# Pooled scores of a unit's two heads: one step that issues both heads' products alternately, in place of a step for each head

## The chip, the cores and the metric

One core of a Trainium2 chip runs the kernel. The metric is the device time of one execution in microseconds; the time before is the median of three runs.

## The reference

Queries, keys and values have 8 batches, 8 heads, 576 positions and 64 features, all in float32. For each head the reference adds up two attentions and then runs a gated feed-forward network (FFN) on the result:

```
q_d, k_d, v_d = mean over 4 neighbouring positions      # 144 pooled positions
out_up  = repeat(softmax(q_d k_d^T / 8) v_d, 4)         # pooled attention
out_loc = softmax(masked q k^T / 8) v                   # only |i - j| < 4
x = out_up + out_loc           # reshaped to 4608 tokens x 512 features
out = (sigmoid(x w_gate) * (x w_val)) w_out             # 512 -> 1536 -> 512
```

The change touches one product only: the pooled scores q_d k_d^T, a 144 x 144 matrix for each head.

## The kernel before

**Attention.** A unit is one batch and a pair of heads, so there are 32 units, numbered 0 to 31, four to a batch. The 64 features of a unit's first head lie on partitions 0 to 63, those of its second head on partitions 64 to 127. `unit_steps` (L414) gives the steps of a unit, each of them a small function: `s0` and `s1` (the local scores, tile `s`, in two parts of 6 and 4 blocks), `sm` (the local softmax), `d0` and `d1` (the pooled scores of the first and of the second head, tile `sd`), `dn` (the pooled softmax's division), `a0` and `a1` (the transposes of the local weights, tile `at`, in two parts), `at` (the transposes of the pooled weights, tile `adt`), `od` (the pooled output), `x` (the local output in two parts, tile `x`, its sum with the pooled output, and the split of the sum into two float16 halves in `xT`).

`s_down(h)` (L505) is the step of one head. It takes a PSUM bank, issues two products of 64 rows, 72 columns and 144 moving columns (`product`, L397), and empties the bank: a maximum on VectorE (L515), its scaling on ScalarE (L516), and two exponentials with their sums on ScalarE (L518). A float32 product stands in the trace as two weight loads and two matmuls, so that a head makes four of each.

**PSUM.** The pool `ps_o` has one bank for each of its tags: `gate`, `val` and `o0` to `o3`, which the FFN uses. The pool `ps_a` has two banks under the tag `att`. The helper `bank` (L449) gives a unit of the first batch the banks `o0` to `o3`; for units 4 to 31 every tile of the attention (`s`, `sd`, `at`, `adt`, `od`, `x`, and `mxt`, the tile of a batch's maximum of the values) comes out of the two `att` banks. A tile can begin when a bank has been emptied by its last reader.

**FFN.** `moe_gate`, `moe_val` and `moe_out` work on 9 chunks of 512 tokens and 12 slices of the hidden width; each call is 12 matmuls of 512 columns. Chunk c needs `xT` of all units of the batches that its tokens come from: chunk 2 needs units 0 to 11, chunk 3 units 0 to 15, and so on to chunk 7, which needs all 32.

**Order.** The table `T` gives each step a position: for units 12 to 31 the unit's base is 82.05 plus 8.17 for each unit after the twelfth, and `m_` entries are offsets from it (L714 to L735). A slice of the FFN takes three positions, one for each of its calls, and `run_steps` puts the attention's steps between the calls. With the offsets of `T` the order in the program is, for a unit and the one before it: `s0`, `a0` of the unit before, `s1`, `d0`, then (once in a batch) `mxt`, then `a1` and `at` of the unit before, `d1`, then `od` and `x` of the unit before. This order is a wish only: the context is opened with `schedule_with_timeline_sim=True` (L866), and so an own timeline of instructions and banks settles, when the program is built, which instruction stands where on each engine. Where a step's bank isn't free in that timeline, FFN matmuls are put ahead of it. On the chip each engine then follows that fixed order and waits where data or a bank isn't ready.

In the first batch, where little other work is there, `awake` adds short matmuls on zeros after some steps (`k_` entries of `T`: three after `d0`, none after `d1`).

Of the kernel before, what the change touches and what calls it, by code (L numbers as in the profile page):

```python
# [16 lines left out]

T = dict(ma=4.5, mas=0.45, mb=9.5, mbs=0.5, c1=56, gs=2.66, g0=16.84, r1=1.99, rs=1.6, ob=3.16, v0=15.13, v1=16.62, v2=17.5, vs=2.12, o0=18, os=1.2, pro=2.36, u4=13.82, u5=21, u6=27, u7=32, l4=1.3, l5=2.77, l6=9.47, l7=8.68, lv=15.08, vm=1.58, b8=6.75, s8=6.63, b12=26.05, s12=8.17, hold=32.07, al=0.76, am=1, z=3.68, sd=0, sn=0.79, v0m=0.61, xd=[2, 3, 7], ad=[0, 3, 7], aa=[0, 1, 2, 3, 6], td=[0, 3, 9, 10], vd=[0, 1, 2, 3, 6, 9, 10], a_prep1=-2.43, a_prep2=-0.89, a_s0=0.01, a_s1=0.52, a_sm=1.82, a_d0=2.39, a_d1=2.6, a_dn=5.17, a_a0=4.37, a_vd=4.6, a_a1=5.1, a_v=2.74, a_at=5.22, a_od=5.79, a_x=8.38, m_prep0=-3.14, m_prep1=-1.14, m_prep2=-1.43, m_s0=0.69, m_s1=2.59, m_sm=3.12, m_d0=2.84, m_d1=5.8, m_a0=10, m_dn=10.78, m_vd=11.67, m_a1=12, m_v=13.07, m_at=13.44, m_od=15.64, m_x=17, k0=30, k_prep1=4, k_prep2=0, k_s0=2, k_s1=2, k_sm=4, k_d0=3, k_d1=0, k_dn=0, k_a0=3, k_vd=8, k_a1=2, k_v=5, k_at=0, k_od=0, k_x=0)  # L20
# [10 lines left out]
SD = S // 4  # L31
QM = SD // 2
# [15 lines left out]
QKSCALE = 1.0 / 8  # L48
# [10 lines left out]
def attention_moe(ctx, tc, qk, qkd, v, vd, wg, wv, wo, mask, out):  # L59
# [234 lines left out]
    vm = {}  # L294
# [119 lines left out]
    def unit_steps(u):  # L414
# [34 lines left out]
        def bank(own, name):  # L449

            if u < NPAIR:
                return ps_o.tile([P, 512], F32, tag=own, name=name)
            return ps_a.tile([P, 512], F32, tag="att", name=name)
# [48 lines left out]
            x = vdraw[u].rearrange("p a b f -> p (a b) f")  # L502
            sum4([(ps, VDB[ps, :, ps]) for ps in HALVES], x, nc.vector if u in T["vd"] else nc.gpsimd)

        def s_down(h):  # L505
            pt = bank(f"o{h}", f"sd_{u}_{h}")
            hs = slice(h * 64, h * 64 + 64)
            for qb in range(2):
                o, rows = pt[:QM, qb * SD : (qb + 1) * SD], slice(qb * QM, (qb + 1) * QM)
                product(o, [s["qd"][hs, rows]], [s["kd"][hs]])  # L510
            if h == 0:
                s["e"] = wk.tile([QM, 2, 2, SD], F32, tag="e", name=f"e_{u}", bufs=1)
                s["sme"] = wk.tile([QM, 4], F32, tag="sme", name=f"sme_{u}")
            mx = wk.tile([QM, 2], F32, tag="mxd", name=f"mxd_{u}_{h}")
            nc.vector.tensor_reduce(mx, pt[:QM, : 2 * SD].rearrange("p (q c) -> p q c", q=2), axis=AX.X, op=ALU.max)  # L515
            nc.scalar.activation(mx, mx, AF.Copy, scale=-QKSCALE / 16)  # L516
            for qb in range(2):
                nc.scalar.activation(s["e"][:, qb, h, :], pt[:QM, qb * SD : (qb + 1) * SD], AF.Exp,  # L518
                                     bias=mx[:, qb : qb + 1], scale=QKSCALE / 16,
                                     accum_out=s["sme"][:, 2 * qb + h : 2 * qb + h + 1])  # L520

        def norm_down():
            own(ad, u)
# [70 lines left out]
        def xsplit():  # L594
# [11 lines left out]

        return dict(
            prep0=lambda: None, prep1=prep1, prep2=prep2, s0=p1, s1=p2, sm=p2b,
            d0=lambda: s_down(0), d1=lambda: s_down(1), dn=norm_down,
            vd=vdsum, v=plain_v if plain else vsplit,  # L610
            a0=lambda: t_local(0, 3), a1=lambda: t_local(3, 5), at=t_down, od=av_down,
            x=lambda: (av_local(0, 8), av_local(8, 10), xsplit()),
# [258 lines left out]
```

## Time and profile before

| | us |
|---|---|
| time, median of 3 runs | 1146.84 |
| the runs | 1142.59, 1146.84, 1147.35 |
| span of the profiled execution | 1140.5 |
| PE (matmul) busy | 1093.5, 96% |
| DVE, ACT, POOL busy | 528.8, 516.9, 335.9 |
| pooled-score matmuls (`sd`) busy | 46.3, 256 instructions |
| share of `sd` in the chain that ended last | 3% |

The span runs from the first to the last instruction of the execution that was profiled; the times of the runs include what lies around it. PE is TensorE's matmuls and PEld its weight loads, DVE is VectorE, ACT is ScalarE, POOL is GpSimd. Matmuls overlap one another, so that a matmul's own duration is longer than the distance to the next one. Where the text speaks of what a matmul costs, it goes by the distance between the starts of successive groups.

### The profile page before, as it was taken

The page shows a single profiled execution, that of the slowest core. Times are in us where ns is not written, and L with a number is a line of the kernel's source. Part 1 is how long each engine was busy: PE and PEld are TensorE (multiplying, and loading weights), DVE is VectorE, ACT ScalarE, POOL GpSimd, SP SyncE. Part 2 cuts the span into 40 slices and gives each one's busy share as a digit, 9 for nine tenths or more (in the row PEclk, how much of TensorE's full clock was granted, in tenths as well). Part 3 has the DMA queues.
Part 4 walks back from the last instruction along what each step waited for, and adds up shares of the span by engine and source line. Part 5 has one row for each costly group of instructions (what it writes and reads, how often), then busy time and mean ns, then how long its engine had stood idle before and what let it go on. Part 6 is the DMA issues. An engine that isn't in the chain of part 4 may idle for free.

```text
span 1140.5 us, 16124 instructions
## 1 busy us (share of the span) xinstructions
PE 1093.5 (96%) x6319; PEld 599.7 (53%) x6319; DVE 528.8 (46%) x956; ACT 516.9 (45%) x1240; POOL 335.9 (29%) x348
## 2 busy tenths in 40 slices
PE   7878779999999999999999999999999999999998
PEld 5754434565555555555555555555555554444443
DVE  6689989744445433444344334433444332122121
ACT  6745666634545444454445444544453432112112
POOL 6334645422333333333323232433233210000000
PEclk8759989999999999999999999999999999999999
DMA  9887766322213211232213221421021000000001
GB/s 367 304 307 279 253 201 207 132 102 83 69 47 123 74 61 66 69 106 69 68 58 105 69 69 35 140 66 61 33 94 36 1 1 37 1 1 38 1 1 37
DMA packets 31900, 110.33 MB, mean 97 GB/s; under 512 B 3536, under 2 KB 3664, under 8 KB 31824
## 3 DMA queue, kind: packets, MB, share of 16 engines
q1 hardware_dynamic: 31824, 109.30, 28.0%
q8 instruction: 50, 0.82, 0.3%
q14 instruction: 26, 0.21, 0.1%
HBM read 99.84 MB, written 9.44 MB: 96 GB/s over the span
## 4 chain that ended last, share of the span: by engine, by line
PE 81%; DVE 3%; DMA 1%; ACT 1%; issue 0%; POOL 0%; DVEq 0%; POOLq 0%
PE po L397 23%; PE pg L397 23%; PE pv L397 22%; PE s L397 5%; PE sd L397 3%; PE x L397 2%; PE od L397 2%; PE at L550 1%; PE adt L560 1%; DMA qk<-in_qk_dram 1%; DMA wo7c<-in_wo_dram 0%; DVE wro L207 0%; DVE wo L158 0%; DVE wro L208 0%; DVE wrg L208 0%
## 5 line engine op out<-in xcount | busy, mean ns | idle before, releaser
L397 PE MATMUL pg<-xT,wg 128*128 128x512 f16 x1296 | 310.6, 383 | 9.2 <-ACT wg L215 5.6
L397 PE MATMUL pv<-xT,wv 128*128 128x512 f16 x1296 | 308.9, 379 | 3.3 <-DVE tanh L637 1.7
L397 PE MATMUL po<-g,wo 128*128 128x512 f16 x1188 | 279.7, 379 | 0.0
L397 PEld LDWEIGHTS <-wg 128*128 128x128 f16 x1296 | 125.2, 99 | 155.3 <-ACT wg L215 7.1
L397 PEld LDWEIGHTS <-wo 128*128 128x128 f16 x1296 | 124.8, 99 | 154.1 <-ACT wo L157 8.7
L397 PEld LDWEIGHTS <-wv 128*128 128x128 f16 x1296 | 125.1, 98 | 144.2 <-issue 4.5
L637 DVE SCALAR_TENSOR_TENSOR tanh<-tanh,pv 128x512 f32<-128x512 f32 x108 | 73.6, 682 | 206.3 <-PE pv L397 202.6
L629 ACT ACTIVATE tanh<-pg,tsc 128x512 f32<-128x512 f32 (+7 forms) x192 | 86.6, 496 | 147.4 <-PE pg L397 147.1
L645 ACT ACTIVATE g<-tanh,gs 128x512 f16<-128x512 f32 x99 | 71.4, 721 | 152.4 <-DVE tanh L637 152.4
L646 DVE SCALAR_TENSOR_TENSOR g<-tanh,gs,g 128x512 f16<-128x512 f32 x99 | 83.9, 847 | 59.0 <-ACT g L645 58.5
L481 POOL TENSOR_TENSOR t<-t,mx 128x640 f32<-128x640 f32 x32 | 43.1, 1346 | 200.1 <-DVE mx L480 196.9
L397 PEld LDWEIGHTS s<-qk,qblk 128*128 128x128 f32 x600 | 76.9, 196 | 9.9 <-ACT qblk L441 2.1
L397 PE MATMUL s<-qk,qblk 128*128 128x64 f32 x600 | 75.7, 276 | 1.9 <-ACT qblk L441 1.6
L603 POOL TENSOR_TENSOR xT<-xs,xT 128x384 f16<-128x384 f32 (+7 forms) x54 | 52.6, 989 | 70.2 <-ACT xT L601 70.1
L469 DVE SCALAR_TENSOR_TENSOR t<-s,mk 128x384 f32<-128x384 f32 x64 | 31.2, 488 | 83.6 <-PE s L397 83.5
L492 POOL TENSOR_TENSOR t<-t,sm 128x640 f32<-128x640 f32 x28 | 36.0, 1287 | 95.2 <-DVE sm L490 92.0
L441 ACT COPY qblk<-qk 64x580 f32<-64x580 f32 x60 | 40.5, 675 | 31.9 <-DMA qk<-in_qk_dram 26.8
L487 DVE TENSOR_REDUCE sm<-t 128x10 f32<-128x640 f32 x32 | 26.2, 817 | 61.1 <-ACT t L482 60.9
L157 ACT ACTIVATE vblk<-v,svb 64x640 f16<-64x640 f32 x48 | 39.5, 824 | 26.8 <-PE x L397 25.9
L516 ACT ACTIVATE mxd<-mxd 72x2 f32<-72x2 f32 x64 | 12.8, 201 | 85.6 <-DVE mxd L515 85.6
L386 POOL TENSOR_TENSOR qkd<-qkd 128x576 f32<-128x576 f32 x29 | 39.2, 1353 | 38.9 <-DMA qkd<-in_qkd_dram 38.7
L515 DVE TENSOR_REDUCE mxd<-sd 72x2 f32<-72x288 f32 x64 | 28.8, 450 | 45.7 <-PE sd L397 45.1
(296 smaller groups left out, 1199.6 us busy)
## 6 DMA issues: line engine op xcount, KB each, us to landing
qk<-in_qk_dram SPq DMA_DIRECT2D x30, 610.0 KB, 3.8
qkd<-in_qkd_dram SPq DMA_DIRECT2D x29, 576.0 KB, 3.7
vd<-in_vd_dram SPq DMA_DIRECT2D x29, 384.0 KB, 3.7
v<-in_v_dram SPq DMA_DIRECT2D x32, 320.0 KB, 2.9
out_dram<-osb SPq DMA_DIRECT2D x16, 512.0 KB, 3.1
wo<-in_qk_dram SPq DMA_DIRECT2D x2, 610.0 KB, 10.5
wo<-in_qkd_dram SPq DMA_DIRECT2D x2, 576.0 KB, 9.3
out_dram<-osb SPq DMA_DIRECT2D x4, 256.0 KB, 2.3
```

The costliest lines, as they stand in the source:

```text
L157: nc.scalar.activation(hi, src, AF.Copy, scale=sc)
L386: nc.gpsimd.tensor_tensor(out=x[:, :, 0:2], in0=x[:, :, 0:2], in1=x[:, :, 2:4], op=ALU.add)
L397: nc.tensor.matmul(o, w[a], x[c], start=first and i == 0, stop=last and i == len(pairs) - 1)
L441: nc.scalar.copy(QB[ps, :, ps.start : ps.start + R], q_[ps])
L469: nc.vector.scalar_tensor_tensor(out=s["t"][:, j0:j1, :], in0=pt[:, : n * 2 * WIN].rearrange("p (a b) -> p a b", a=n), scalar=QKSCALE, in1 ...
L481: nc.gpsimd.tensor_tensor(out=t, in0=t, in1=mx.unsqueeze(2).to_broadcast([P, NBLK, WIN]), op=ALU.subtract)
L492: eng.tensor_tensor(out=t, in0=t, in1=sm.unsqueeze(2).to_broadcast([P, NBLK, WIN]), op=ALU.mult)
L603: eng.tensor_tensor(out=x[:, hp, 1, o : o + n], in0=src, in1=x[:, hp, 0, o : o + n], op=ALU.subtract)
L629: nc.scalar.activation(t[:, o : o + n], pt[:, o : o + n], AF.Tanh, scale=tsc[:, b, fc : fc + 1])
L637: nc.vector.scalar_tensor_tensor(out=t, in0=t, scalar=1.0, in1=pt, op0=ALU.add, op1=ALU.mult)
L645: nc.scalar.activation(g[:, 0], t, AF.Copy, scale=gs[:, fc : fc + 1])
L646: nc.vector.scalar_tensor_tensor(out=g[:, 1], in0=t, scalar=gs[:, fc : fc + 1], in1=g[:, 0], op0=ALU.mult, op1=ALU.subtract)
```

## The change

`d0` becomes the step of both heads. It takes two banks, issues the first query half of head 0, the first half of head 1, the second half of head 0 and the second half of head 1, and then empties the two banks, head 0 first. `d1` disappears, and with it its entries in `T` (`a_d1`, `m_d1`, `k_d1`). No other entry is altered, so head 1's pooled scores move from offset 5.8 to offset 2.84, from behind `a1` and `at` of the unit before to a place ahead of them. Number, shape and type of all instructions stay as they are.

```diff
-T = dict(... a_d0=2.39, a_d1=2.6, ... m_d0=2.84, m_d1=5.8, ... k_d0=3, k_d1=0, ...)
+T = dict(... a_d0=2.39, ... m_d0=2.84, ... k_d0=3, ...)
...
-        def s_down(h):
-            pt = bank(f"o{h}", f"sd_{u}_{h}")
-            hs = slice(h * 64, h * 64 + 64)
+        def s_down():
+            pts = [bank(f"o{h}", f"sd_{u}_{h}") for h in range(2)]
+            heads = [slice(h * 64, h * 64 + 64) for h in range(2)]
             for qb in range(2):
-                o, rows = pt[:QM, qb * SD : (qb + 1) * SD], slice(qb * QM, (qb + 1) * QM)
-                product(o, [s["qd"][hs, rows]], [s["kd"][hs]])
-            if h == 0:
-                s["e"] = wk.tile([QM, 2, 2, SD], F32, tag="e", name=f"e_{u}", bufs=1)
-                s["sme"] = wk.tile([QM, 4], F32, tag="sme", name=f"sme_{u}")
-            mx = wk.tile([QM, 2], F32, tag="mxd", name=f"mxd_{u}_{h}")
-            nc.vector.tensor_reduce(mx, ...)
-            nc.scalar.activation(mx, mx, AF.Copy, scale=-QKSCALE / 16)
-            for qb in range(2):
-                nc.scalar.activation(s["e"][:, qb, h, :], ...)
+                rows = slice(qb * QM, (qb + 1) * QM)
+                for pt, hs in zip(pts, heads):
+                    product(pt[:QM, qb * SD : (qb + 1) * SD], [s["qd"][hs, rows]], [s["kd"][hs]])
+            s["e"] = wk.tile([QM, 2, 2, SD], F32, tag="e", name=f"e_{u}", bufs=1)
+            s["sme"] = wk.tile([QM, 4], F32, tag="sme", name=f"sme_{u}")
+            for h, pt in enumerate(pts):
+                mx = wk.tile([QM, 2], F32, tag="mxd", name=f"mxd_{u}_{h}")
+                nc.vector.tensor_reduce(mx, ...)
+                nc.scalar.activation(mx, mx, AF.Copy, scale=-QKSCALE / 16)
+                for qb in range(2):
+                    nc.scalar.activation(s["e"][:, qb, h, :], ...)
...
-            d0=lambda: s_down(0), d1=lambda: s_down(1), dn=norm_down,
+            d0=s_down, dn=norm_down,
```

## Rows read from the trace of the kernel before

**Rows 1.** The page: span, and each engine's busy time with its share.

```profile
span 1140.5 us, 16124 instructions
PE 1093.5 (96%) x6319; PEld 599.7 (53%) x6319; DVE 528.8 (46%) x956; ACT 516.9 (45%) x1240; POOL 335.9 (29%) x348
```

**Rows 2.** Windows: stretch, length; busy PE, PEld, DVE, ACT, POOL; PE clock, DMA.

```profile
160.00:200.00 40.00, 31.59 (x143) 15.00 (x142) 38.37 (x64) 27.46 (x56) 22.29 (x12) 0.87 0.58 189
240.00:300.00 60.00, 60.00 (x342) 32.11 (x341) 28.73 (x58) 30.40 (x81) 15.60 (x16) 1.00 0.24 79
300.00:400.00 100.00, 98.07 (x639) 55.76 (x638) 44.25 (x83) 48.31 (x123) 35.79 (x42) 1.00 0.25 83
500.00:600.00 100.00, 100.00 (x632) 54.79 (x630) 40.83 (x77) 45.27 (x113) 34.20 (x40) 1.00 0.22 71
```

**Rows 3.** Timeline of PE from 9 us, unit 0: start, length, instructions.

```profile
10.27 0.72 PE L397 MATMUL sd<-qks 64*72 64x144 f32 x8
10.92 1.26 PE L76 MATMUL awake<-idle 128*128 128x256 bf16 x6
```

**Rows 4.** Timeline of PE, 663 to 696 us, same columns: the attention's groups.

```profile
664.47 1.00 PE L397 MATMUL s<-qk,qblk 128*128 128x64 f32 x8
665.40 0.71 PE L397 MATMUL sd<-qks 64*72 64x144 f32 x4
666.04 1.69 PE L397 MATMUL pg<-xT,wg 128*128 128x512 f16 x7
667.57 2.75 PE L397 MATMUL pv<-xT,wv 128*128 128x512 f16 x12
670.16 0.38 PE L550 MATMUL at<-ident,t 128*128 128x128 f32 x2
...
671.45 0.55 PE L560 MATMUL adt<-ident,ad 72*128 72x72 f32 x6
...
675.94 0.38 PE L397 MATMUL pv<-xT,wv 128*128 128x512 f16 x1
676.25 0.71 PE L397 MATMUL sd<-qks 64*72 64x144 f32 x4
676.88 1.00 PE L397 MATMUL od<-adt,vdblk 128*128 128x144 f32 x6
...
682.26 0.98 PE L397 MATMUL x<-at,vblk 128*128 128x58 f16 x30
...
687.82 1.45 PE L397 MATMUL s<-qk,qblk 128*128 128x64 f32 x12
689.11 0.50 PE L550 MATMUL at<-ident,t 128*128 128x128 f32 x3
...
693.97 1.00 PE L397 MATMUL s<-qk,qblk 128*128 128x64 f32 x8
694.90 0.71 PE L397 MATMUL sd<-qks 64*72 64x144 f32 x4
```

**Rows 5.** Timeline of all engines, 664 to 668.5 us: two banks being emptied.

```profile
665.51 0.42 DVE L469 SCALAR_TENSOR_TENSOR t<-s,mk 128x256 f32<-128x256 f32 x1 [1.99 <-PE s L397]
...
667.56 0.19 ACT L518 ACTIVATION_READ_ACCUMULATOR e<-sd,mxd 72x1 f32 x1
```

**Rows 6.** Groups by line: busy, mean ns of one, idle before.

```profile
L637 DVE SCALAR_TENSOR_TENSOR tanh<-tanh,pv 128x512 f32<-128x512 f32 x108 | 73.6, 682 | 206.3 <-PE pv L397 202.6 <-PE mxt L126 3.1 <-ACT tanh L629 0.4
...
L158 DVE SCALAR_TENSOR_TENSOR vblk<-v,svb,vblk 64x640 f16<-64x640 f32 x48 | 45.0, 937 | 2.0 <-issue 0.6
```

**Rows 7.** Timeline of PE, 714 to 726 us: chunk 4 begins.

```profile
715.42 0.98 PE L397 MATMUL x<-at,vblk 128*128 128x58 f16 x30
716.24 1.24 PE L397 MATMUL pv<-xT,wv 128*128 128x512 f16 x5
...
721.53 0.81 PE L397 MATMUL pg<-xT,wg 128*128 128x512 f16 x3
```

**Rows 8.** Timeline of PE, 359 to 368 us: chunk 2 begins; idle time before in brackets.

```profile
361.26 0.38 PE L131 MATMUL mxt<-mxg,ones 1*128 1x1 f32 x2 [0.61 <-DVE mxg L130]
361.88 0.97 PE L397 MATMUL x<-at,vblk 128*128 128x58 f16 x30 [0.25 <-DVE pvb L143]
363.50 0.71 PE L397 MATMUL sd<-qks 64*72 64x144 f32 x4 [0.64 <-DVE sxb L308]
```

More of the change, by code (lines that the diff above doesn't have):

```diff
@@ L16 @@
 PSUM = bass.MemoryType.PSUM
-T = dict(ma=4.5, mas=0.45, mb=9.5, mbs=0.5, c1=56, gs=2.66, g0=16.84, r1=1.99, rs=1.6, ob=3.16, v0=15.13, v1=16.62, v2=17.5, vs=2.12, o0=18, os=1.2, pro=2.36, u4=13.82, u5=21, u6=27, u7=32, l4=1.3, l5=2.77, l6=9.47, l7=8.68, lv=15.08, vm=1.58, b8=6.75, s8=6.63, b12=26.05, s12=8.17, hold=32.07, al=0.76, am=1, z=3.68, sd=0, sn=0.79, v0m=0.61, xd=[2, 3, 7], ad=[0, 3, 7], aa=[0, 1, 2, 3, 6], td=[0, 3, 9, 10], vd=[0, 1, 2, 3, 6, 9, 10], a_prep1=-2.43, a_prep2=-0.89, a_s0=0.01, a_s1=0.52, a_sm=1.82, a_d0=2.39, a_d1=2.6, a_dn=5.17, a_a0=4.37, a_vd=4.6, a_a1=5.1, a_v=2.74, a_at=5.22, a_od=5.79, a_x=8.38, m_prep0=-3.14, m_prep1=-1.14, m_prep2=-1.43, m_s0=0.69, m_s1=2.59, m_sm=3.12, m_d0=2.84, m_d1=5.8, m_a0=10, m_dn=10.78, m_vd=11.67, m_a1=12, m_v=13.07, m_at=13.44, m_od=15.64, m_x=17, k0=30, k_prep1=4, k_prep2=0, k_s0=2, k_s1=2, k_sm=4, k_d0=3, k_d1=0, k_dn=0, k_a0=3, k_vd=8, k_a1=2, k_v=5, k_at=0, k_od=0, k_x=0)
+T = dict(ma=4.5, mas=0.45, mb=9.5, mbs=0.5, c1=56, gs=2.66, g0=16.84, r1=1.99, rs=1.6, ob=3.16, v0=15.13, v1=16.62, v2=17.5, vs=2.12, o0=18, os=1.2, pro=2.36, u4=13.82, u5=21, u6=27, u7=32, l4=1.3, l5=2.77, l6=9.47, l7=8.68, lv=15.08, vm=1.58, b8=6.75, s8=6.63, b12=26.05, s12=8.17, hold=32.07, al=0.76, am=1, z=3.68, sd=0, sn=0.79, v0m=0.61, xd=[2, 3, 7], ad=[0, 3, 7], aa=[0, 1, 2, 3, 6], td=[0, 3, 9, 10], vd=[0, 1, 2, 3, 6, 9, 10], a_prep1=-2.43, a_prep2=-0.89, a_s0=0.01, a_s1=0.52, a_sm=1.82, a_d0=2.39, a_dn=5.17, a_a0=4.37, a_vd=4.6, a_a1=5.1, a_v=2.74, a_at=5.22, a_od=5.79, a_x=8.38, m_prep0=-3.14, m_prep1=-1.14, m_prep2=-1.43, m_s0=0.69, m_s1=2.59, m_sm=3.12, m_d0=2.84, m_a0=10, m_dn=10.78, m_vd=11.67, m_a1=12, m_v=13.07, m_at=13.44, m_od=15.64, m_x=17, k0=30, k_prep1=4, k_prep2=0, k_s0=2, k_s1=2, k_sm=4, k_d0=3, k_dn=0, k_a0=3, k_vd=8, k_a1=2, k_v=5, k_at=0, k_od=0, k_x=0)
 P = 128
@@ L503, in vdsum @@
             sum4([(ps, VDB[ps, :, ps]) for ps in HALVES], x, nc.vector if u in T["vd"] else nc.gpsimd)
-        def s_down(h):
-            pt = bank(f"o{h}", f"sd_{u}_{h}")
-            hs = slice(h * 64, h * 64 + 64)
+        def s_down():
+            pts = [bank(f"o{h}", f"sd_{u}_{h}") for h in range(2)]
+            heads = [slice(h * 64, h * 64 + 64) for h in range(2)]
             for qb in range(2):
-                o, rows = pt[:QM, qb * SD : (qb + 1) * SD], slice(qb * QM, (qb + 1) * QM)
-                product(o, [s["qd"][hs, rows]], [s["kd"][hs]])
-            if h == 0:
-                s["e"] = wk.tile([QM, 2, 2, SD], F32, tag="e", name=f"e_{u}", bufs=1)
-                s["sme"] = wk.tile([QM, 4], F32, tag="sme", name=f"sme_{u}")
-            mx = wk.tile([QM, 2], F32, tag="mxd", name=f"mxd_{u}_{h}")
-            nc.vector.tensor_reduce(mx, pt[:QM, : 2 * SD].rearrange("p (q c) -> p q c", q=2), axis=AX.X, op=ALU.max)
-            nc.scalar.activation(mx, mx, AF.Copy, scale=-QKSCALE / 16)
-            for qb in range(2):
-                nc.scalar.activation(s["e"][:, qb, h, :], pt[:QM, qb * SD : (qb + 1) * SD], AF.Exp,
-                                     bias=mx[:, qb : qb + 1], scale=QKSCALE / 16,
-                                     accum_out=s["sme"][:, 2 * qb + h : 2 * qb + h + 1])
+                rows = slice(qb * QM, (qb + 1) * QM)
[5 more added lines that the diff above has]
+                mx = wk.tile([QM, 2], F32, tag="mxd", name=f"mxd_{u}_{h}")
+                nc.vector.tensor_reduce(mx, pt[:QM, : 2 * SD].rearrange("p (q c) -> p q c", q=2), axis=AX.X, op=ALU.max)
+                nc.scalar.activation(mx, mx, AF.Copy, scale=-QKSCALE / 16)
+                for qb in range(2):
+                    nc.scalar.activation(s["e"][:, qb, h, :], pt[:QM, qb * SD : (qb + 1) * SD], AF.Exp,
+                                         bias=mx[:, qb : qb + 1], scale=QKSCALE / 16,
+                                         accum_out=s["sme"][:, 2 * qb + h : 2 * qb + h + 1])
         def norm_down():
@@ L732, in attention_moe @@
             add(p0 + offset(u, k), units[u][k])
-            if b == 0 and T["k_" + k] and k in ("s0", "s1", "d0", "d1", "a0", "a1", "at", "od", "x"):
+            if b == 0 and T["k_" + k] and k in ("s0", "s1", "d0", "a0", "a1", "at", "od", "x"):
                 add(p0 + offset(u, k), lambda n=T["k_" + k]: awake(n))
```

## The prediction

> **What bounds the kernel.** I read the page first: PE is busy for 96% of the span, every other engine for less than half [rows 1]. That is an average, so the windows come next. Up to about 240 us, where weights are converted, VectorE is the busier one (38.4 of 40 us between 160 and 200, PE 31.6). From 240 us on PE has work in all of the time but for a few us, at the full clock (100.0 of 100 us between 500 and 600) [rows 2]. Units 8 to 31, 24 of the 32, run in this second part: there a microsecond of PE time saved is a microsecond of the whole, and one of any other engine is nothing unless PE ends up waiting for it. So the timeline of PE is the view that decides. It has each unit's pooled scores twice, as groups of four matmuls, some 11 us apart (665.40 and 676.25) [rows 4].
>
> **What a joined group would save.** An FFN call of 12 matmuls goes from 667.57 to 670.16, 0.216 us each. A group `sd` of one head holds PE from 665.40 to 666.04, 0.64 us, and the FFN matmul ahead of the other one holds it for 0.31 us (675.94 to 676.25), 0.09 more than its share [rows 4]. One head thus costs 0.73 us, two cost 1.46. Unit 0 shows the two heads side by side: eight matmuls in 0.65 us (10.27 to 10.92), hardly more than four elsewhere [rows 3]. The heads use different halves of the array's rows, and here they plainly ran at the same time. Joined, a unit costs 0.65 + 0.09 = 0.74, and **0.72 us** is saved. All 24 units would give 17.3 us.
>
> Nothing is removed or added, so this saving is the only direct one, and it needs the heads to be neighbours on PE. That they alternate matters less: unit 0's code issues head 0's products first, then head 1's, and yet they overlapped. The Trainium skill says otherwise (TensorE: Matmul & The Clock Gate, Part 3, what overlaps and what doesn't): matmuls start and end strictly in program order. By that rule the change's order, two matmuls a head in turn, would overlap only where the head changes, five steps in place of four, and save some 0.56 us a unit; unit 0's 0.65 us speak against it.
>
> **Whether the heads become neighbours** is the real question. The order on PE is fixed ahead by the kernel's own timeline, and the trace shows what that timeline waits for. At 665.51 the second local score's bank is being emptied, which takes 0.42 us, and the head's bank is empty by 667.75 [rows 5]; yet the next users of these two banks stand at 670.16 and 671.45 [rows 4]. So on the chip there are several us to spare, and the planned order holds each bank for some 5.4 to 6.2 us from one user to the next. Reading these holds off the starts in rows 4: first local scores to second 6.15 (687.82 to 693.97); first `at` to `sd` 5.79 (689.11 to 694.90); second local scores to second `at` 5.69 (664.47 to 670.16); `sd` to `adt` 6.05; second `at` to `sd` 6.09; `adt` to `od` 5.43; `od` to `x` 5.38; `x` to the next scores 5.56.
>
> Now I walk the changed order with these holds, two banks, each step taking the bank that is free first. `od` waits for `adt`'s data and the first part of `x` for `adt`'s bank, so both come at 0. The second part of `x` takes `od`'s bank at 5.38. The next unit's first scores take the other at 5.56, the first `at` comes at 5.38 + 5.56 = 10.94, the second scores at 5.56 + 6.15 = 11.71. Head 0 gets its bank at 10.94 + 5.79 = 16.73, **head 1 at 11.71 + 5.69 = 17.40**. The second `at` follows at 22.78, `adt` at 23.45, the next `od` at 28.88. Two readings follow. The period is 28.9 us, against 29.5 before (665.40 to 694.90): the chain of banks gets no longer, so attention reaches the FFN about as early as now. And head 1 is ready 0.67 us after head 0. In that time head 0's two products take two places in the order, 0.43 us at an FFN matmul's 0.216; then, with head 1 not ready, the timeline puts FFN matmuls between, and the unit costs what it cost before.
>
> That 0.67 is not exact. Each release can stand behind one VectorE instruction of other work, 0.68 to 0.94 us [rows 6], so I take a gap anywhere from 0 to 1.6 us (0.67 + 0.94); the heads are neighbours where it is under 0.43, in 0.43 / 1.6 = 27% of the units. I take 6.5 of 24: 6.5 x 0.72 = **4.7 us** gained. The bounds are 0 and 17.3 us.
>
> **The rest.** Units 0 to 7: PE isn't the bound there [rows 2], unit 0 is joined already; I take 0, with bounds of 3 us either way (four units at 0.72 as a gain, the same as a loss by a changed order). Head 1's maximum, scaling and exponentials move with it: the same instructions on VectorE and ScalarE, some 8 us earlier, behind head 0's. They lengthen the hold of head 1's bank by up to head 0's own time on the two engines (2.2 us, 665.51 to 667.75); only `adt` or `a1` waits for that bank, and the walk has 0.6 us of its period to give, so up to 1.6 us a unit is a possible loss of pace, on the side of rival 2; I take 0, because what it delays stands ahead of the FFN by the cover priced there. POOL's pooling of the next unit waits for head 1's products to have been read, and is let go earlier: no cost. No DMA is issued by the step. The clock stays at 1.00 where PE is full [rows 2].
>
> The profile's own span is 1140.5 us [rows 1] and the median of the runs 1146.8, 6.3 more; neither start nor end is touched, so the same stands around the span afterwards: 1140.5 - 4.7 = 1135.8, plus 6.3, is **1142 us**.
>
> **Rivals.**
> (1) *The heads join in most units.* For it: the walk misses by only 0.24 us (0.67 against 0.43), and the timeline's holds may differ from the ones I read by more. Against it: a delay on either bank parts them. Four fifths of 24 units give 19 x 0.72 = 13.8 us, so 1133.
> (2) *Attention comes late to the FFN, and it gets slower.* Both heads now sit in the only two banks, so nothing else of the attention starts until head 0 is out. If that makes the chain longer by one hold (5.4 us or more) in each batch, the cover is gone: at the start of chunk 4 the last unit's `x` ends at 716.24, and the first matmuls that need it stand at 721.53, 5.3 us of other work [rows 7]. Where that cover is missing now, at chunk 2, PE idles 0.61 + 0.25 + 0.64 = 1.5 us around `x` [rows 8]. Chunks 2 to 7 have such a start: 6 x 1.5 = 9 us at the least, 6 x 5.4 = 32 at the most; nearer the first, since banks turn over fast once PE has nothing queued: about 12, hence 1158. It decides from the point where a batch of four units takes 5.3 us more than before; the walk has it 2.4 us shorter (4 x 0.6), and a batch's `mxt` tile, which I left out, lies between. The Trainium skill warns of this side (TensorEngine Tiling (Array Packing), Gotcha 1: PSUM Pressure): row tiles running together need a bank each, which raises the pressure on PSUM.
> (3) *It doesn't do what it says:* the timeline parts the heads in every unit. Then the times of before stand, 1147.
>
> **Chances.** The forecast (2 to 11 units joined) 0.44, rival 1 0.27, rival 2 0.17, rival 3 0.12. A measurement of this kernel tells some 0.5%, 5.7 us, from no change, so faster means below 1141.1. Rival 1 and the better third of the forecast (0.13) give faster 0.40; slower takes nearly all of rival 2, 0.16; the same is left with 0.44. Range: rival 1 with nearly all units reaches 1130; above, the lesser part of rival 2 reaches 1156. The forecast's own range is 1139 to 1147.
>
> **What would show it.** In the timeline of PE, groups `sd` of eight matmuls that hold it some 0.65 us in about a quarter of units 8 to 31, and groups of four with FFN matmuls between in the others; right after the second local scores comes head 0. PE's busy time should fall by about 5 us, with no new idle time at 664 to 912 us. Eights nearly everywhere speak for rival 1; idle time of PE ahead of `x`, `pg` or `pv` where a chunk begins speaks for rival 2; no eights after 240 us for rival 3. I am wrong on the mechanism if eights are there and hold PE for 1.2 us.

## The result

| us | before | after |
|---|---|---|
| time, median of 4 runs | 1147.09 (1142.59 to 1147.45) | 1133.54 (1132.31 to 1134.72) |
| span of the profiled execution | 1140.5 | 1132.2 |
| its mean granted TensorE clock | 0.973 | 0.971 |

The ratio is 0.9876, with a 95% interval of 0.9834 to 0.9918: the kernel became faster by 13.6 us. The profiled executions differ by only 8.3 us, because the one of before was among its fastest; at an equal granted clock the gain is some 10 us, as the experiments show.

The page of after, to be read against [rows 1]: PE's busy time is nearly what it was (1093.5), so the 8.3 us of span are mostly time in which PE stood idle.

```profile
span 1132.2 us, 16161 instructions
PE 1092.7 (97%) x6319; PEld 601.4 (53%) x6319; DVE 523.8 (46%) x956; ACT 516.8 (46%) x1240; POOL 319.8 (28%) x348
```

The windows say where it was idle. The columns are those of [rows 2]; first before, in two stretches not shown so far, then after, in these two and in the one from 300 to 400 us, which [rows 2] has of before.

```profile
0.00:240.00 240.00, 200.19 (x1074) 125.17 (x1075) 194.90 (x352) 144.23 (x333) 115.34 (x98) 0.87 0.71 250
160.00:240.00 80.00, 70.60 (x378) 39.28 (x377) 65.07 (x110) 49.04 (x103) 37.37 (x24) 0.94 0.47 157
```

```profile
0.00:240.00 240.00, 206.70 (x1111) 131.18 (x1112) 193.51 (x358) 150.28 (x351) 105.32 (x101) 0.88 0.71 255
160.00:240.00 80.00, 74.86 (x404) 41.46 (x405) 65.07 (x105) 50.50 (x110) 28.61 (x25) 0.98 0.48 165
300.00:400.00 100.00, 98.31 (x615) 55.47 (x614) 43.48 (x84) 51.41 (x131) 34.12 (x39) 0.97 0.26 84
```

Before 240 us PE was idle for 39.8 us and is now for 33.3; that is 6.5 us, and 4.3 of them lie between 160 and 240. There the clock rose too, from 0.94 to 0.98. Between 300 and 400 it fell from 1.00 to 0.97. Another 2.3 us lie in the first 60 us, where after was granted less (0.77 against 0.80) and PE was busy for longer, 51.1 us against 48.7; these are not to be taken for a gain.

A second view says the same from the other end. VectorE's products on the hidden values are twelve to a chunk; the first one of chunk 1 and the last one of all mark the stretch in which PE is full. Timeline of DVE, before and after, these two rows:

```profile
244.33 0.69 DVE L637 SCALAR_TENSOR_TENSOR tanh<-tanh,pv 128x512 f32<-128x512 f32 x1
...
1130.55 0.69 DVE L637 SCALAR_TENSOR_TENSOR tanh<-tanh,pv 128x512 f32<-128x512 f32 x1 [5.54 <-PE pv L397]
```

```profile
237.49 0.69 DVE L638 SCALAR_TENSOR_TENSOR tanh<-tanh,pv 128x512 f32<-128x512 f32 x1
...
1122.61 0.69 DVE L638 SCALAR_TENSOR_TENSOR tanh<-tanh,pv 128x512 f32<-128x512 f32 x1 [5.54 <-PE pv L397]
```

The stretch begins 6.8 us earlier and is 886.2 us long before, 885.1 after: 1.1 us of the 8.3 come from the part that the prediction argued about, 6.8 from the part that it set to nothing. A second profile of the same kernel (the run called "after, once more" below) has 236.43 and 1120.48 for these rows, so 7.9 and 2.2 us.

**The joined units.** Two looks at PE's timeline of after, one unit each, with the columns of [rows 4]:

```profile
716.34 0.49 PE L551 MATMUL at<-ident,t 128*128 128x128 f32 x3
716.66 1.00 PE L397 MATMUL s<-qk,qblk 128*128 128x64 f32 x8
...
722.56 0.71 PE L397 MATMUL sd<-qks 64*72 64x144 f32 x8
723.21 0.39 PE L397 MATMUL pv<-xT,wv 128*128 128x512 f16 x1
...
738.37 1.89 PE L397 MATMUL pv<-xT,wv 128*128 128x512 f16 x8
740.10 0.32 PE L397 MATMUL x<-at,vblk 128*128 128x58 f16 x6
740.26 1.53 PE L397 MATMUL s<-qk,qblk 128*128 128x64 f32 x12
...
743.79 0.49 PE L551 MATMUL at<-ident,t 128*128 128x128 f32 x3
...
746.49 1.00 PE L397 MATMUL s<-qk,qblk 128*128 128x64 f32 x8
...
749.36 0.71 PE L397 MATMUL sd<-qks 64*72 64x144 f32 x4
750.00 2.12 PE L397 MATMUL pv<-xT,wv 128*128 128x512 f16 x9
752.05 0.71 PE L397 MATMUL sd<-qks 64*72 64x144 f32 x4
```

The first unit of a batch has its eight matmuls together and they hold PE for 0.65 us (722.56 to 723.21). The second has two groups of four, 0.64 us each, with nine FFN matmuls between. There are four such eights after 240 us (at 486.9, 604.8, 722.6 and 840.3 us, the first units of batches 4 to 7); the other 20 units look like the second one, with 2.0 to 4.9 us from the start of one head to that of the other. One of these, unit 8, has its heads just ahead of 240 us, at 233.3 and 235.4.

**Where PE no longer waits.** PE's waits between 60 and 240 us by line and releaser (us in all, times, longest), first before, then after:

```profile
PE po L397 <- ACT wo L157: 7.5, 3, 5.7
PE pg L397 <- ACT wg L215: 5.6, 3, 3.8
```

```profile
PE pg L397 <- ACT wg L215: 6.4, 3, 3.4
...
PE po L397 <- ACT wo L157: 1.2, 2, 0.8
```

The largest wait for converted weights, 5.7 us long, is gone. PE's timeline around it, before and after:

```profile
161.01 0.71 PE L397 MATMUL sd<-qks 64*72 64x144 f32 x4
167.40 3.60 PE L397 MATMUL po<-wo 128*128 128x512 f16 x8 [5.69 <-ACT wo L157]
170.79 0.63 PE L550 MATMUL at<-ident,t 128*128 128x128 f32 x2
...
174.97 0.54 PE L560 MATMUL adt<-ident,ad 72*128 72x72 f32 x6
...
175.56 1.00 PE L397 MATMUL s<-qk,qblk 128*128 128x64 f32 x8
```

```profile
159.50 0.38 PE L551 MATMUL at<-ident,t 128*128 128x128 f32 x2
161.06 0.60 PE L561 MATMUL adt<-ident,ad 72*128 72x72 f32 x6 [1.17 <-ACT at L543]
162.48 1.10 PE L397 MATMUL s<-qk,qblk 128*128 128x64 f32 x8 [0.83 <-DVE t L469]
163.51 0.71 PE L397 MATMUL sd<-qks 64*72 64x144 f32 x4
164.65 3.54 PE L397 MATMUL po<-wo 128*128 128x512 f16 x8 [0.43 <-ACT wo L157]
```

Before, `po` stands in PE's order right behind the second head of unit 6 (161.01) and waits for `wo`; by the order of the program unit 5's second `at`, its `adt` and unit 7's second scores stand behind it and have to wait too. After, unit 6's second head came at 136.2, the steps that take the banks behind it stand earlier in the order, and those same groups are ahead of `po`: PE does them while the weights are being converted.

### The profile page after: what moved, and what is told of

It reads as the page before. It is cut to its first block, busy times and chain, and to the rows that moved or that the text cites. A ratio compares the mean times of both kernels' runs of the same rounds, so it can differ in the third digit from the quotient of the medians.

```text
span 1132.2 us, 16161 instructions
## 1 busy us (share of the span) xinstructions
PE 1092.7 (97%) x6319; PEld 601.4 (53%) x6319; DVE 523.8 (46%) x956; ACT 516.8 (46%) x1240; POOL 319.8 (28%) x348
## 4 chain that ended last, share of the span: by engine, by line
PE 85%; DVE 5%; DMA 5%; ACT 3%; issue 1%; POOL 0%; SPq 0%; DVEq 0%; ACTq 0%; POOLq 0%
PE po L397 23%; PE pv L397 23%; PE pg L397 23%; PE s L397 6%; PE x L397 3%; PE sd L397 3%; PE od L397 2%; PE at L551 2%; PE adt L561 1%; DMA wv<-in_vd_dram 1%; DVE wrg L208 1%; DMA wv1m<-in_wv_dram 1%; DVE wrg L209 1%; DMA vd<-in_vd_dram 1%; DMA qk<-in_qk_dram 1%
## 5 line engine op out<-in xcount | busy, mean ns | idle before, releaser
L397 PE MATMUL pv<-xT,wv 128*128 128x512 f16 x1296 | 313.3, 383 | 6.2 <-POOL wv L216 2.3
L647 DVE SCALAR_TENSOR_TENSOR g<-tanh,gs,g 128x512 f16<-128x512 f32 x99 | 80.0, 808 | 66.5 <-ACT g L646 66.0
L397 PE MATMUL s<-qk,qblk 128*128 128x64 f32 x600 | 78.7, 281 | 2.9 <-ACT qblk L441 1.5
L604 POOL TENSOR_TENSOR xT<-xs,xT 128x384 f16<-128x384 f32 (+7 forms) x54 | 50.1, 931 | 87.0 <-ACT xT L602 86.9
L593 DVE TENSOR_TENSOR xs<-x,od 128x464 f32<-128x464 f32 (+1 forms) x56 | 25.0, 455 | 100.9 <-PE x L397 95.1
L388 POOL TENSOR_TENSOR vdblk<-vd 64x192 f32<-64x192 f32 x50 | 28.2, 563 | 89.1 <-PE od L397 87.1
L386 POOL TENSOR_TENSOR qkd<-qkd 128x576 f32<-128x576 f32 x29 | 34.4, 1188 | 60.6 <-DMA qkd<-in_qkd_dram 50.8
L158 DVE SCALAR_TENSOR_TENSOR vblk<-v,svb,vblk 64x640 f16<-64x640 f32 x48 | 46.1, 960 | 9.8 <-ACT vblk L157 8.9
L536 POOL TENSOR_TENSOR ad<-e,sme 72x288 f32<-72x288 f32 x52 | 35.4, 699 | 49.4 <-PE adt L561 45.2
L519 ACT ACTIVATE e<-sd,mxd 72x144 f32<-72x144 f32 x128 | 47.0, 370 | 2.0 <-POOL t L481 0.4
```

The lines of the kernel that those rows point to most:

```text
L158: nc.vector.scalar_tensor_tensor(out=lo, in0=src, scalar=sc, in1=hi, op0=ALU.mult, op1=ALU.subtract)
L386: nc.gpsimd.tensor_tensor(out=x[:, :, 0:2], in0=x[:, :, 0:2], in1=x[:, :, 2:4], op=ALU.add)
L397: nc.tensor.matmul(o, w[a], x[c], start=first and i == 0, stop=last and i == len(pairs) - 1)
L536: eng.tensor_tensor(out=AD[:, qb].rearrange("p c h k -> p h c k")[:, :, :, :KC], in0=s["e"][:, qb].rearrange("p h (c k) -> p h c k", c=NKC ...
L604: eng.tensor_tensor(out=x[:, hp, 1, o : o + n], in0=src, in1=x[:, hp, 0, o : o + n], op=ALU.subtract)
L647: nc.vector.scalar_tensor_tensor(out=g[:, 1], in0=t, scalar=gs[:, fc : fc + 1], in1=g[:, 0], op0=ALU.mult, op1=ALU.subtract)
```

## The experiments

Each ran beside the kernel before; a ratio is to that. The letters of theories belong to each expectation alone. One thing about comparing them has to come first. Times of one kernel on one chip differ by up to 1.1% with the granted clock: beside one of the runs, before took a span of 1143.2 us at a mean clock of 0.968 and 1153.9 at 0.956. A straight line through the spans of 130 executions, all whose clock is on record, with a level for each kernel (on each chip for before) and one slope, gives -0.73 us for each 0.001 of mean clock, and leaves a scatter of 1.6 us. The levels at clock 0.968 compare kernels more finely than the medians do; they are spans, some 1.8 us shorter than times. They take out also what a kernel gains or loses in clock by its own doing. So the gains that they show are a little too small for the early part (0.94 to 0.98 over 80 us is 0.003 of the mean, some 2 us), and too large where a kernel lost clock at chunk 2 (0.97 over 100 us in after, some 2 us as well).

| kernel | median, us | ratio (95%) | executions | level of the span at 0.968, us | less than before on the same chip |
|---|---|---|---|---|---|
| before (four chips) | 1147 to 1149 | | 53 | 1144.9 to 1146.6 | |
| after | 1133.54 | 0.9876 (0.9834, 0.9918) | 4 | 1135.0 | 9.9 to 11.6 (its chip is not on record) |
| after, once more | 1134.90 | 0.9898 (0.9851, 0.9944) | 4 | 1135.4 | 10.4 |
| joined step in units 0 to 7 | 1135.92 | 0.9891 (0.9861, 0.9922) | 4 | 1136.7 | 8.2 |
| in units 8 to 31 | 1143.03 | 0.9946 (0.9916, 0.9975) | 10 | 1141.9 | 3.0 |
| in units 4 to 7 | 1134.43 | 0.9882 (0.9850, 0.9914) | 4 | 1136.1 | 9.7 |
| in units 0 to 3 | 1144.21 | 0.9975 (0.9952, 0.9999) | 10 | 1143.6 | 2.2 |
| in unit 6 | 1143.77 | 0.9957 (0.9924, 0.9991) | 10 | 1141.7 | 3.8 |
| before, head 1 a little earlier | 1136.45 | 0.9912 (0.9884, 0.9939) | 10 | 1138.5 | 7.0 |
| before, head 1 right behind head 0 | 1139.49 | 0.9923 (0.9898, 0.9948) | 5 | 1135.9 | 9.0 |
| after, units 8 to 31 held together | 1132.38 | 0.9857 (0.9828, 0.9886) | 4 | 1128.8 | 16.1 |
| the same, 2.6 positions later | 1135.71 | 0.9881 (0.9838, 0.9924) | 4 | 1130.5 | 15.2 |
| the same, units 8 to 11 moved | 1132.35 | 0.9859 (0.9806, 0.9912) | 4 | 1129.4 | 16.0 |
| after, units 16 to 31 held together | 1131.23 | 0.9828 (0.9757, 0.9898) | 4 | 1131.3 | 15.3 |

By the scatter a level of 4 executions is good to about 1.6 us.

**Which units the gain is in.** Two kernels have the joined step in one part of the units and the two steps of before in the rest.

```
-            d0=s_down, dn=norm_down,
+            d0=s_down if u < 8 else lambda: s_one(0),
+            d1=(lambda: None) if u < 8 else lambda: s_one(1), dn=norm_down,
```

> The joined step for units 0 to 7 alone; units 8 to 31 keep the two steps of before. Theory A (the gain is PE's idle time ahead of 240 us, which the moved steps of the first units shorten by some 7 us, and 0.72 us for each unit after that whose heads are neighbours, 4 units): most of the gain stays, 1147 - 7 = 1140, between 1138 and 1142, and PE's idle time ahead of 240 us is near the 33 us of the changed kernel, not the 41 of before. Theory B (the gain lies in the attention of units 8 to 31, by neighbouring heads or by a shorter chain of banks): nearly nothing stays, 1145 to 1148.

```
-            d0=s_down, dn=norm_down,
+            d0=s_down if u >= 8 else lambda: s_one(0),
+            d1=(lambda: None) if u >= 8 else lambda: s_one(1), dn=norm_down,
```

> The joined step for units 8 to 31 alone; units 0 to 7 keep the two steps of before. Theory A: 4 units with neighbouring heads at 0.72 us, so 2.9 us less than before, 1144, between 1142 and 1146, with PE's idle time ahead of 240 us as before, 41 us. Theory B: nearly the whole gain, 1133 to 1136.

Units 0 to 7 alone gave 1135.92, below what was expected for them; units 8 to 31 alone gave 1143.03, as expected, with four eights as in after. At equal clock 8.2 and 3.0 us make 11.2, the change's 10.4 within the scatter. Most of the gain lies where the prediction had put nothing. The two parts are not quite apart, though. With units 0 to 7 joined the planned order of the later units moved too, though their steps are those of before: PE is idle for 0.3 us between 300 and 400, where before has 1.9 and after 1.7, and the stretch marked by VectorE's products is 883.7 us long, 2.6 less than before. So some of the 8.2 us lies behind 240 us.

The expectations go by PE's idle time ahead of 240 us as well (39.8 us in before by the windows). It tells less than the times do: 32.1 with units 0 to 7 joined, but also 35.7 with units 8 to 31, whose early steps are those of before. There PE was granted 0.76 in the first 60 us and was busy for 52.2 of them, against 48.7 at 0.80 in before. The stretch from 160 to 240 is the better measure.

**Which of the early units.** The same edit for units 4 to 7, for units 0 to 3, and for unit 6 alone:

```
+            d0=s_down if 4 <= u < 8 else lambda: s_one(0),
+            d1=(lambda: None) if 4 <= u < 8 else lambda: s_one(1), dn=norm_down,
```

> The joined step for units 4 to 7 alone, which run while the FFN's first chunk waits for converted weights; units 0 to 3 and 8 to 31 keep two steps. Theory A1 (the early gain is attention work of units 4 to 7 that fills PE's waits for weights between 80 and 240 us): as with units 0 to 7 joined, 7 to 8 us below before at the same clock. Theory A2 (it is the start, units 0 to 3, ahead of 60 us): within 2 us of before at the same clock. If it is merely that any new order is a better one: in between, with no pattern.

```
+            d0=s_down if u < 4 else lambda: s_one(0),
+            d1=(lambda: None) if u < 4 else lambda: s_one(1), dn=norm_down,
```

> The joined step for units 0 to 3 alone. Theory A1: within 2 us of before at the same clock. Theory A2: 5 to 8 us below before at the same clock. PE's idle time ahead of 240 us should be near 40 us by A1, near 33 by A2.

```
+            d0=s_down if u == 6 else lambda: s_one(0),
+            d1=(lambda: None) if u == 6 else lambda: s_one(1), dn=norm_down,
```

> The joined step for unit 6 alone, the unit whose second head stood 30 us behind its first (131.3 and 161.0 us) and held up the pooled and local output of unit 5 behind it. Theory A1, in its narrow form (this one late step is what left PE without attention work while it waited for weights): most of the gain of units 4 to 7, 5 to 9 us below before at the same clock, and unit 5's x done near 181 us, not 202. If each of the four units gives its share: 2 us or so. If it is any new order: anything.

Units 4 to 7 gave 1134.43, nearly all of the change and a little more than expected; units 0 to 3 gave 1144.21, 2.2 us at equal clock. The windows from 160 to 240 us (columns of [rows 2]) of the first and the second of these:

```profile
160.00:240.00 80.00, 75.32 (x408) 41.84 (x407) 65.62 (x111) 50.89 (x105) 27.88 (x24) 0.98 0.46 158
```

```profile
160.00:240.00 80.00, 70.63 (x378) 39.33 (x376) 64.53 (x107) 50.20 (x104) 35.31 (x25) 0.94 0.50 159
```

With units 4 to 7 joined PE is busy for 75.3 of the 80 us at 0.98, with units 0 to 3 for 70.6 at 0.94, as before. Unit 6 alone brought 3.8 us at equal clock, less than was expected, though its longest wait for `wo` is 1.5 us and no longer 5.7, and PE was busy for 73.71 us in that stretch, 3.1 us more than before of the 4.3 that after has more. So the one wait doesn't price the gain; what the units beside it add isn't taken apart.

**Is it the joining, or only the order?** Nothing is joined here: in the kernel before, head 1's position alone is altered, by 0.3 of a position (an FFN call).

```
-T = dict(... m_d1=5.8, ...)
+T = dict(... m_d1=5.5, ...)
```

> The kernel before with one number of T altered a little: m_d1 5.5 for 5.8, no joined step. In the order of PE the second heads of units 6 and 7 come some 30 and 18 matmuls sooner, units 0 to 5 are as before. A control for how much of a gain any small shift of that step gives. Theory A1: as unit 5's output still stands behind unit 6's second head, up to a third of the gain, 0 to 3 us at the same clock. If any change of order is as good: 6 us or more.

It gave 1136.45, 7.0 us less than before at equal clock, against what was expected. PE's waits from 60 to 240 us have the same line gone, and the timeline shows the same groups ahead of `po`, which comes 0.8 us later than the end of its wait before but finds the attention done:

```profile
PE po L397 <- ACT wo L157: 2.0, 3, 0.8
```

```profile
163.39 0.59 PE L560 MATMUL adt<-ident,ad 72*128 72x72 f32 x6 [1.82 <-ACT at L542]
165.14 1.97 PE L397 MATMUL s<-qk,qblk 128*128 128x64 f32 x8 [1.15 <-DVE t L469]
167.04 1.23 PE L397 MATMUL sd<-qks 64*72 64x144 f32 x4
168.20 3.59 PE L397 MATMUL po<-wo 128*128 128x512 f16 x8
```

Unit 6's second head comes at 153.6 here, 161.0 before and 136.2 after. Its profiled execution had the clock of before's (0.973), so that the two spans compare as they are: 1134.6 us, 5.9 less, of which 4.1 lie ahead of chunk 1's first product (240.23 against 244.33) and 1.8 behind it. So two thirds of the gain need no joined heads: a shift gives them that lets the attention of units 5 to 7 stand ahead of the waiting `po`. Whether the last third comes from joining or from a better order still, no run shows.

**Is it the alternation?** Again before, with head 1's step put right behind head 0's, so that each head's products stay together in their own step:

```
-T = dict(... a_d1=2.6, ... m_d1=5.8, ...)
+T = dict(... a_d1=2.4, ... m_d1=2.85, ...)
```

> The kernel before with only two numbers of T altered: the second head's step right behind the first's (m_d1 2.85 for 5.8, a_d1 2.4 for 2.6). Two steps, one bank each, head 0's products first, no alternation. Theory A (the place of the second head's step is what matters, not that its products alternate): like the changed kernel, 1133 to 1136. If alternating or taking both banks in one step matters by itself: 1140 to 1147.

Its median of 1139.49 lies between the two ranges expected. But its executions fell on a lower clock (0.965 in the middle, as those of before on that chip), and at equal clock it is at 1135.9, the change at 1135.0 and 1135.4. It has four eights too, at the same units, in its program with head 0's four matmuls ahead of head 1's:

```profile
731.06 0.72 PE L397 MATMUL sd<-qks 64*72 64x144 f32 x8
731.72 0.39 PE L397 MATMUL pv<-xT,wv 128*128 128x512 f16 x1
```

They hold PE for 0.66 us (731.06 to 731.72), against 0.65 alternated. The trace has the single matmuls of both kernels in pairs, 14 ns apart here (731.064 and 731.078, then 731.244 and 731.258), 7 ns apart in after (722.561 and 722.568); so they ran two at a time in both. It doesn't name a matmul's head; that one order is by head and the other alternates is taken from the programs. The order of the products is worth at most 0.01 us a unit; what the change does, it does by its placement, as far as a scatter of 1.6 us tells.

**The change once more**, beside other executions of before and without an edit:

> The changed kernel once more, beside the runs that follow, for a comparison on one chip. No theory separates here: 1132 to 1138, the middle of it where the clock is low for longer.

It gave 1134.90, and 1135.4 at equal clock, the level of the first time (1135.0).

**What full joining is worth.** From here on the heads of late units are made neighbours. One column of the first bank is written by VectorE first, so that the bank is taken before the products come, and the other three products are tied to the first of head 1, which needs the second bank:

```
+            if u >= PINNED:   # 8
+                nc.vector.memset(pts[0][:QM, :1], 0.0)
+                first = mm(0, 1)
+                with tc.issue_after(first.ins):
+                    mm(0, 0), mm(1, 1), mm(1, 0)
```

> The changed kernel, with the heads of units 8 to 31 made neighbours: a one-column memset by VectorE takes the first bank, and the other three products are queued behind the one that takes the second bank. Nothing else differs, one memset a unit apart. Theory A's price, 0.72 us a unit, for the 20 units that are not joined in the changed kernel: 14.4 us less, 1133.5 - 14.4 = 1119, between 1116 and 1123, groups of eight matmuls that hold PE for 0.65 us in all 24 units. If overlap were a matter of unit 0's stretch alone (PE empty, other banks), the eights would hold PE for 1.1 to 1.2 us and the time would fall by 5 us at most, the drains saved: 1128 to 1134. If holding the first bank longer makes attention late for the FFN: new idle time where chunks begin, 1133 or more.

All 24 units have their eights, and the kernel took 1132.38 us, 9 more than the upper end of what was expected. PE's `sd` matmuls after 240 us are busy for 17.4 us and were for 34.0 before, 0.69 us less in each of 24 units (29.8 in after, for 23 units), so the joined heads pay what the prediction said. But PE now waits; its waits after 240 us by line and releaser:

```profile
PE s L398 <- DVE xs L600: 2.3, 4, 0.7
PE mxt L127 <- ACT e L526: 1.7, 1, 1.7
PE pg L398 <- POOL xT L611: 0.8, 3, 0.4
```

These and five smaller ones make 7.2 us, against 1.7 in after; 4.7 us lie between 300 and 400, around the start of chunk 2, where the clock falls as well:

```profile
300.00:400.00 100.00, 95.28 (x615) 55.24 (x613) 42.58 (x84) 48.96 (x121) 34.58 (x41) 0.95 0.26 80
```

At 0.95 some 10 of these 100 us ran at 1.2 GHz, and with PE busy that is 5 us of work lost. From the first to the last of VectorE's products, taken as above, there are 879.1 us (244.43 to 1123.49), 6.0 less than in after. Its early part, 6.9 us longer than in after (244.43 against 237.49), hides that in its span of 1133.1 us; that part is the same code, and its clock was 0.85 in the first 240 us, 0.88 in after. At equal clock the kernel is some 6 us below the change.

Two kernels tried to put work in front of chunk 2: all joined steps later, and the units of batch 2 earlier.

```
-T = dict(... m_d0=2.84, ...)
+T = dict(... m_d0=5.4, ...)
```

> The kernel with neighbouring heads in units 8 to 31 (e4_pinned), with the joined step at offset 5.4 in place of 2.84 (m_d0), behind the transposes of the unit before. If what the neighbours save (13 us of PE time) is partly paid back because both banks are held while the unit before still needs its own: less idle time of PE where chunks begin than the 7.2 us after 240 us of e4_pinned, and 2 to 5 us less at the same clock. If the idle time there comes from something else: the same time as e4_pinned within 2 us, or more, since the first units' order changes too.

```
-T = dict(... b8=6.75, ...)
+T = dict(... b8=12, ...)
```

> Neighbouring heads in units 8 to 31 (e4_pinned) with units 8 to 11 begun 5.25 positions sooner (b8 12 for 6.75). If e4_pinned pays part of its saving back because the attention of units 8 to 11 comes late for chunk 2, PE's idle time between 300 and 400 us falls from 4.7 to 1 us or less and the time by 2 to 4 us at the same clock. If the idle time there has another cause: the same time as e4_pinned within 2 us.

Neither gained: 1135.71 and 1132.35, and 1130.5 and 1129.4 at equal clock, against 1128.8. In the first PE's idle time after 240 us grew to 8.4 us, 5.4 of them between 400 and 500. In the second the idle time left chunk 2 and came back at chunk 3:

```profile
300.00:400.00 100.00, 100.00 (x637) 53.78 (x636) 41.77 (x80) 47.78 (x117) 31.79 (x36) 1.00 0.21 69
400.00:500.00 100.00, 94.77 (x584) 52.42 (x583) 40.45 (x85) 49.57 (x128) 30.99 (x37) 0.97 0.26 85
```

The last one leaves units 8 to 15 as in after and holds only the heads of units 16 to 31 together:

```
-PINNED = 8
+PINNED = 16
```

> The joined heads held as neighbours only in units 16 to 31, units 8 to 15 left as in the changed kernel. All as in the run that pins units 8 to 31, but the first eight of them. Theory A: the idle time of about 5 us stands at the first chunk whose units are pinned (chunk 2 with units 8 to 31 pinned, chunk 3 where unit 8's base was later), because a pinned unit asks for both banks at once and its batch ends later: it moves to chunk 4, about 5 us between 560 and 620, and the whole gains no more than the run with all pinned did: about 6 us below the changed kernel at equal clock or less. Theory B: the idle time belongs to the early batches, whose attention has little work behind it, and not to pinning: from chunk 4 on only 0.4 to 0.7 us a chunk is lost, so idle time after 240 us stays under 4 us and the 12 or 13 more joined units give 8 us, less 2 us: at equal clock 6 to 8 us below the changed kernel, with fewer units pinned.

The 5 us of idle time didn't move on to chunk 4, where 0.9 us stand between 560 and 620. After 240 us it is 4.3 us in all, a little over what its second theory allowed; the windows from 300 us on:

```profile
300.00:400.00 100.00, 98.12 (x622) 54.91 (x621) 43.31 (x83) 49.99 (x122) 34.05 (x40) 0.98 0.26 83
400.00:500.00 100.00, 100.00 (x617) 54.32 (x616) 41.30 (x81) 48.41 (x126) 33.06 (x38) 1.00 0.23 75
500.00:600.00 100.00, 99.07 (x648) 55.70 (x647) 40.78 (x84) 48.09 (x116) 31.61 (x38) 1.00 0.24 76
```

So the 5 us belong to holding heads together in batches 2 and 3; in the later ones it costs 0.7 to 0.9 us a chunk. The kernel has the lowest median, 1131.23, and 879.0 us from VectorE's first product to its last, with 16 eights, where the kernel with 24 of them has 879.1. Its gain over before on the same chip is 4.9 us more than the change's (15.3 against 10.4). That is the time of the first theory (6 us or less) and not of the second (6 to 8), while the place of the idle time is that of the second; with a scatter of this size the time doesn't decide. At equal clock the four kernels with heads held together beat before and the change; by their medians alone they can't be told from the change, whose runs overlap with theirs.

## Why the prediction was right, and where it was wrong

The time of 1133.54 lies in the range of 1130 to 1156, but below the likeliest case's own range of 1139 to 1147, and not by the reasons given: it is what rival 1 would give, and rival 1's mechanism (heads joined in most units) is not there. That the range holds the time is luck. Most of the gain comes from a term that the sum has at 0, units 0 to 7.

**What a joined unit saves: right.** Eights hold PE for 0.65 us and fours for 0.64, as read off unit 0 [rows 3] and [rows 4]. That alternation matters less than being neighbours was right as well: 0.65 against 0.66 us. By the strict order of the Trainium skill (TensorE: Matmul & The Clock Gate, Part 3, what overlaps and what doesn't) four matmuls of one head followed by four of the other should overlap only at the seam, and the trace disagrees, if PE got them in the order of the program: eight in 0.66 us, started in pairs.

**How many units join: mechanism right, size off.** Four, not 6.5 of 24, so 2.9 us and not 4.7. By the order of the starts the walk failed in one hold. It let both parts of `x` keep their banks for 5.38 and 5.56 us. In the timeline of after the second, smaller part comes at 740.10, and the first `at` takes its bank at 743.79, 3.69 later. With that the first `at` stands 2.70 us ahead of the second scores (743.79 and 746.49), where the walk had 0.77 (10.94 and 11.71), and the heads come 2.69 us apart, not 0.67. The other holds were right: first to second scores 6.23 (6.15), `at` to `sd` 5.57 (5.79), scores to `sd` 5.56 (5.69). The four units that join are the first of a batch, where `at` and scores stand 0.32 us apart (716.34 and 716.66). A chance of 27% spread over all units was the wrong picture: in the last four batches one unit in four joins, always the first.

**The late part: the saving is there, and the clock took most of it back.** The 2.9 us show as only 1.1 between VectorE's first and last product. At chunk 2 PE ran for 6.8 us at 1.2 GHz in after, half of its speed elsewhere in the stretch, which loses some 3.4 us of work, where before lost none (0.97 and 1.00 over 100 us). Take each kernel's stretch, less PE's waits in it and half of the time at 1.2 GHz; that estimates PE's work at full clock. It is 880 us in after (885.1 - 1.7 - 3.4), and 880 too in its second profile and in the kernels with the joined step in units 8 to 31 and with head 1 right behind head 0; it is 883 to 884 in before (886.2 - 2.3) and in the five other kernels with two steps apart in units 8 to 31. So 3 to 4 us are saved, as 2.9 says. All four profiles of kernels with the four eights lost clock at chunk 2, 1.7 to 3.4 us by this count, and none of the six profiles without: a cost that came with this order of the late units each time and that the prediction left out ("the clock stays at 1.00 where PE is full"). Why the clock fell behind after's 1.7 us of waits and not behind before's 1.9 stays open. Another suspect is cleared: `x` now stands in two groups (24 and 6 matmuls) with FFN matmuls between, where one group of 30 stood before [rows 7], but the eight FFN matmuls ahead of the second group take 0.216 us each (738.37 to 740.10), with nothing added.

**Units 0 to 7: the term that was mis-sized.** It stood at 0 with 3 us either way, because PE isn't the bound there. It was 6.8 and 7.9 us ahead of chunk 1's first product in the two profiles of after; the kernels with the joined step in early units alone gained 8.2 and 9.7 us at equal clock, of which 2.6 and 2.1 lie behind that product in their profiles. The sentence was true and the conclusion false: where PE waits for converted weights, its time depends on what stands behind the waiting `po` in its order, and the change altered that order. The row was there to be seen: 31.59 busy of 40 us between 160 and 200 [rows 2]. I read it as "VectorE is the busier one" and did not ask what work was ready and stuck behind the wait. PE's waits in that stretch, by line, would have shown one of 5.7 us, and the attention right behind it.

**What lies around the span: wrong by its reading.** 6.3 us were the difference between the profiled execution of before and the median of others. What lies around the span is 1.85 us (1134.05 for the execution with a span of 1132.2). The other 4.4 fit a clock that was better than in most of its executions (0.973, against 0.965 to 0.968 in the middle of those beside the other runs). It explains why the medians differ by 5 us more than the profiles.

**The sum, mended**, as an estimate. For the profiled executions: idle time of PE 42.1 before and 35.0 after (39.8 and 33.3 up to 240 us, 1.9 and 1.7 from 300 to 400, 0.4 in before at 724), so -7.1; four joined units -2.9; the clock 0.973 and 0.971, where the part missing from 1, times the span, is 30.8 and 32.8 us, so +2.0. That gives -8.0; measured -8.3. (The clock's term counts also time in which PE had nothing to do.) PE's busy time fell by only 0.8 us, not by the 5 that the prediction names as a sign: the lower clock in the first 60 us and at chunk 2 made other work longer.

**Rival 2** named a true mechanism that this change hardly sets off. In after the lost cover showed as 1.7 us idle at chunk 2, no more than the 1.9 before (1.5 of them in [rows 8]). Where all units hold both banks together it costs 7.2 us, the largest part of it at chunk 2, at `mxt` and `x`, as in [rows 8]; then it moves from chunk 2 to chunk 3 with the batch, and from chunk 4 on it takes 0.7 to 0.9 us a chunk. (The stretch that [rows 7] and this rival call the start of chunk 4 is that of chunk 5: of VectorE's twelve products a chunk the 61st stands at 724.36 before, the 49th at 603.64. The 5.3 us of cover are read rightly. And 12 us more than 1146.8 are 1159, not 1158.) The warning of the Trainium skill (TensorEngine Tiling (Array Packing), Gotcha 1: PSUM Pressure) is borne out by that kernel's 7.2 us. **Rival 3** (nothing joins) is true of 20 of the 24 units; its time of 1147 misses the early gain, as the forecast does.

## What to carry to other kernels

Where an engine works in program order and waits for something slow, the price of a change of order is read from what stands behind that wait, even if the engine isn't the bound there: list its waits in that stretch and ask which ready work each of them blocks. Before a gain is credited to what an edit says it does, move a part of it without the rest: here a shift of one unjoined step by 0.3 positions gave two thirds of what the joined step did. And compare kernels at the same granted clock, or with many executions: the single profiled execution of before lay some 4.4 us off the median.

## What the runs showed of the hardware

The time of an execution goes with the clock that it was granted, kernel by kernel, by 0.73 us for 0.001 of the mean. What is granted differs from one execution to the next, most of all in the first 60 us. There before was granted 0.80 in its profiled execution, and the kernel with the joined step in unit 6 alone, whose steps up to there are those of before, 0.68 (windows, columns of [rows 2]):

```profile
0.00:60.00 60.00, 48.72 (x301) 39.93 (x302) 39.65 (x83) 43.03 (x123) 28.38 (x35) 0.80 0.88 335
```

```profile
0.00:60.00 60.00, 50.98 (x271) 41.79 (x272) 34.14 (x68) 39.97 (x115) 27.75 (x34) 0.68 0.83 316
```

A group of 64-row matmuls among the FFN's adds to the matmul ahead of it, and groups of 72 and 128 rows add nothing. Between 420 and 900 us in after an FFN matmul ahead of `sd` (64 rows) holds PE for 0.309 us, in all 30 places, and one ahead of `adt` (72 rows) or of `x`, `s`, `at` or `od` (128 rows) for 0.216, as one ahead of another FFN matmul does.

The clock can make a short wait dearer than its length. Behind the waits at chunk 2, 1.7 us in all, PE ran for 6.8 us at 1.2 GHz in after and for 3.4 in its second profile; in before, with 1.9 us of waits there, it stayed at 2.4 GHz (1.00) [rows 2]. In after twelve matmuls of the first local scores are spread over 2.82 us behind the wait at chunk 2, and over 1.53 elsewhere (740.26). PE's timeline there:

```profile
355.27 1.15 PE L397 MATMUL x<-at,vblk 128*128 128x58 f16 x30 [0.40 <-ACT e L519]
356.93 2.82 PE L397 MATMUL s<-qk,qblk 128*128 128x64 f32 x12 [0.52 <-DVE xs L593]
```
